# Chunk 0's transpose moved from the end of a phase to its start, in a two-layer Fourier and MLP kernel

## The chip, the cores and the metric

The kernel runs on one core of a Trainium2 chip. The core has a matrix engine (TensorE, called PE in the profile, with its weight loads as PEld), a vector engine (VectorE, DVE), a scalar engine (ScalarE, ACT), GpSimd (POOL) and a queue engine (SyncE, SP) which here issues the DMAs. The engines run side by side and wait for each other by semaphores. The metric is the device time of one execution in microseconds (us). The time before is 1433.97 us, the median of three runs (1433.92 to 1434.22).

## The reference

The sequence has 2048 rows of 512 numbers. Two kinds of layer alternate, each twice, in float32:

```
A(x): a = x @ Wd_re^T ; b = x @ Wd_im^T            # DFT along the 512
      y = Ws_re @ a - Ws_im @ b                     # DFT along the 2048, real part
B(x): h  = gelu(layernorm(x) @ w1)
      hs = [h shifted +1 | -1 | +2 | -2 rows, a quarter of the columns each] @ w2
      x1 = x + hs
      return x1 + gelu(layernorm(x1) @ w3) @ w4
x = x + A(layernorm(x)) ; x = x + B(layernorm(x))   # twice
```

So B works on a layernorm of a layernorm of x; the kernel calls that twice normed and transposed block `z`. It is the input of the product with w1.

## The kernel before

The 2048 rows are cut in NC = 4 chunks of 512 rows (CH), a chunk in TC = 4 tiles of 128 rows. `xs[0..7]` keep two tiles each in SBUF, and `xt(j)` is tile j of 16. All products are float32 in three passes (`mm3`, L279 to L281): each operand is split into a rounded high part and a low rest, and high x high, high x low and low x high are summed. A high part is a cast on ACT (`high`, L423; L225, L228, L232 for streamed pieces), a low part a subtraction on DVE (`low`, L426; L242). Three matmuls of 512 columns thus use one pair of blocks, and the second of the three (L280) is the first that reads the low part of the streamed block.

The DFT matrices and the weights come from HBM piece by piece. `issue_dma` (L207) queues a load into one of RAW = 4 `raw` buffers as soon as the buffer's last reader is done; `stage_one` takes a ring slot, and casts; `stage_two` makes the low part. There are RING = 4 ring slots. `stream()` hands the next split piece to the matmuls and first calls `prefetch`, which writes as many stages as ring slots are free. All of it is written in one program order (a manual schedule): on each engine the instructions run in the order in which the Python code emits them, and SP's queue holds the loads in that order too. A load or store that waits holds all that is queued behind it.

A layer's chunk c of the sequence DFT has an x phase (`x_phase`, steps i = 0 to 15, two for each of 8 pairs k) and a y phase (`y_phase`, two kinds for each of 8 k, `by1` and `by0`). In the y phase a piece of the stream is the difference of two raw pieces: DVE subtracts them (`ring0f` to `ring3f`, L231), ACT casts the difference (L232), DVE makes the low part (L242). One k takes four such DVE operations and uses two raw buffers. Each kind feeds 12 matmuls into two of the PSUM pairs PA to PD. At a phase's steps a `hook` emits other work: loads, norms, statistics, transposes. After the last chunk's y phase the products along the 512 follow (`hid`, four of them in HORDER, on the blocks `rr`), and then `by_pairs`, which multiplies by w1 and w2 and runs the MLP. Its first product reads z of chunk 0 from `zt[0]` (f32 name `zt0f`), whose words are those of `ay0`, `ay1` and the start of `ay5`, operands of the y phase.

Getting z of a chunk into `zt` has five parts: four norms on ACT (`normed_act`, L327, into `tmp`, `spare` or `extra`), four transposes on DVE in blocks of 32 x 32 (`turn_one`, L591, into `turned`), four stores of 256 KB to a DRAM buffer `zd` (`turn_out`, L601), one load of 1024 KB in the order that finishes the transpose (`turn_in`, L606), and the split into high and low (`z_half`). `edges(0)` then clears two columns at zt's border (a memset on DVE, L611). z of chunk 0 goes this way late in the last chunk (c = 3) of each layer; z of chunk 1 follows at once in `by_pairs`, through the tile `turned01`. The scheduled stores of other work also use SP: `w4s<-w4sum` (L1445, a sum of w4 blocks that is made at x steps 10 and 11 in `w4_sum`, words 5*AY on) and the loads of `xs` from DRAM at x steps 8, 11 and 13 (BACK).

Of the kernel before, what the change touches and what calls it, by code (L numbers as in the profile page):

```python
# [19 lines left out]
CH = 512  # L20
# [22 lines left out]
def spectral_mlp_kernel(ctx: ExitStack, tc: tile.TileContext, x, ws, hs, w1, w2, w34, out):  # L43
# [50 lines left out]
    w12 = [at(f"w12{i}", W12 + i * 4 * CH, 2, 2, CH) for i in range(4)]  # L94
    beside = at("beside", XS - 4 * D - 2 * HALO * KD * 2, 4, D, dtype=F32)
    xs = [at(f"xs{i}", XS + i * 2 * D, 2, D, dtype=F32) for i in range(NP)]
    turned01 = at("turned01", H3, KD, CH, dtype=F32)
    spare = at("spare", SPARE, 2, D, dtype=F32)
    (re0, im0), (re1, im1) = ([both(f"rr{i}{h}", RR + (2 * i + h) * 4 * CH, 2, 2, CH) for i in range(2)] for h in range(2))
# [628 lines left out]
    def by_pairs(layer, zs, xin, dst):  # L728
        act = nc.scalar.copy
        w1p = [stream(), stream()]  # L730
        edges(0)
        for q in range(TC):
            turn_one(turned01, q, zs[4 + q])
# [713 lines left out]
    for layer in range(LAYERS):  # L1447
# [4 lines left out]
        for c in range(NC):  # L1452
            if layer == 0 and c == 0:
                raws[0] = raw_at[0]
                for i in (1, 0):
                    load_x()
                    nc.sync.dma_start(raws[0][:, i], pieces[0][0][:, i])
                state["dma"] += 1
                issue_dma(2)
                load_x()  # L1460
                issue_dma()
                load_x()

                slots[0] = ring[0]
                state.update(one=1, made=1)

                def block_high(i):
                    nc.scalar.copy(ring[0][:, i, 0], raws[0][:, i])

                def block_low(i):  # L1470
                    nc.vector.tensor_tensor(
                        ring[0][:, i, 1], raws[0][:, i], ring[0][:, i, 0].bitcast(F32), op=ALU.subtract
                    )

                def second_low(i):
                    nc.vector.tensor_tensor(
                        ring[1][:, i, 1], raws[1][:, i], ring[1][:, i, 0].bitcast(F32), op=ALU.subtract
                    )

                halves = [pairs[0][:, i].rearrange("p (h d) -> p h d", h=2) for i in range(2)]  # L1480
                parts = [
                    [(halves[0][:, 1], mid[0][:, 0], 1), (halves[0][:, 0], ay[0][:, 2], 0)],
                    [(halves[1][:, 0], mid[0][:, 1], 0), (halves[1][:, 1], ay[0][:, 3], 1)],
                ]

                def part_highs(i):
                    for _, t, h in parts[i]:
                        normed(t[:, 0], xt(i)[:, h * DH : (h + 1) * DH], xp[0][i])

                def part_lows(i):  # L1490
                    for v, t, _ in parts[i]:
                        nc.vector.tensor_tensor(t[:, 1], v, t[:, 0].bitcast(F32), op=ALU.subtract)

                xp[0] = stats([xt(0)])
                block_high(1)
                block_low(1)
                part_highs(0)
                normed_act(pairs[0][:, 0], xt(0), xp[0][0])
                block_high(0)
                xp[0] += stats([xt(1)])  # L1500
                part_lows(0)
                part_highs(1)
                normed_act(pairs[0][:, 1], xt(1), xp[0][1])
                block_low(0)
                state["two"] += 1
                issue_dma()
                part_lows(1)
                xp[0] = pairs[0]
                state["limit"] = 2

                def hook(i):
                    k, odd = divmod(i, 2)
                    if not i:
                        second_low(1)
                        xp_stats(1)
                        second_low(0)
                        state["two"] += 1
                        issue_dma()
                        state["limit"] = 4
                        prefetch()  # L1520
                    state["limit"] = w_items[layer]
                    if not odd:
                        if k + 1 < NP:
                            xp_norm(k + 1, 3)
                            xp_main(k + 1)
                        if not k:
                            xp_main_lows(1)
                    else:
                        if 0 < k < NP - 1:
                            xp_main_lows(k + 1)  # L1530
                        if k + 2 < NP:
                            xp_stats(k + 2)
                        if k:
                            xp_sums(k - 1)
                            xp_highs(k - 1, False)
                            xp_lows(k - 1, False)
                    w4_split(i)

                plain_phase(hook)
                continue  # L1540

            def hook(i):
                k, odd = divmod(i, 2)
                if layer == 0 and c == 1:
                    if i == 1:
                        xp_sums(NP - 1)
                    if i == 2:
                        xp_highs(NP - 1, False)
                    if i == 3:
                        xp_lows(NP - 1, False)  # L1550
                    w4_split(2 * NP + i)
                if c == 0:
                    if layer:
                        for step, f in zip((0, 0, 1), (ay_sums, ay_highs, ay_lows)):
                            if i == step:
                                f(5)
                            if i == step + 10:
                                f(6)
                        for k, first, stages in (
                            (6, X6, (xp_stats, xp_norm, ax_sums, ax_highs, ax_lows)),  # L1560
                            (7, X7, (xp_stats, xp_norm, ax_sums, ax_highs, ax_lows)),
                        ):
                            for step, f in zip((0, 1, 3, 4, 6), stages):
                                if i == first + step:
                                    f(k)
                    return
                if (layer, c) in W4_AT:
                    w4_sums(W4_AT[layer, c], i)
                j = (c - 1) * TC
                if i == 4:  # L1570
                    rows(X1, xin, j, 2, True)
                if i == 9:
                    rows(X1, x1d, j, 2, False)
                if i == 10:
                    rows(X1, xin, j + 2, 2, True)
                if c == NC - 1 and i in BACK:
                    rows(xs[BACK[i] // 2], x1d, BACK[i], 2, True)

            x_phase(c, hook)

            def hook(k):
                if layer and c == 0:
                    for step, f in zip((1, 1, 2), (ay_sums, ay_highs, ay_lows)):
                        if k == step:
                            f(7)
                if k == 1 and c:
                    rows(X1, x1d, (c - 1) * TC + 2, 2, False)
                if c == NC - 1:
                    if k < 2:
                        for j in (2 * k, 2 * k + 1):  # L1590
                            zs[j] = tmp[:, j]
                            normed_act(zs[j], xt(j), ln2[j])
                    if k in (3, 4):
                        for q in (2 * k - 6, 2 * k - 5):
                            turn_one(turned01, q, zs.pop(q))
                    if k == NP - 2:
                        turn_out(turned01)

            y_phase(c, hook)

# [4 lines left out]
        for i, (ri, dp) in enumerate(HORDER):  # L1605
            if i == 1:
                run_late("im1")
            if i == 3:
                state["limit"] += 2
            s = stream()  # L1610
            hid(ri, dp, s, acc4, 0, i == 0, i == 3)
            if i == 0:
                turn_in(ztf[0], HALO)
            if i < 2:
                j = (6, 8)[i]
                rows(xs[j // 2], x1d, j, 2, True)
            if i == 0:
                run_late("re1", "im1+")
            if i == 1:
                run_late("re0+", "re0++")  # L1620
                for half in range(2):
                    high(z_half(0, half))
                zs.update(norm_z((4, 5)))
            if i == 2:
                run_late("re0")
                for half in range(2):
                    low(z_half(0, half))
                zs.update(norm_z((6, 7)))
        by_pairs(layer, zs, xin, out if last_layer else x2d)


# [53 lines left out]
```

## Time and profile before

| | |
|---|---|
| median of the runs | 1433.97 us |
| the profiled execution | 1435.09 us, its span 1433.0 us |
| PE busy | 1426.2 us, 100% of the span, 6285 matmuls |
| PEld, DVE, ACT, POOL busy | 82%, 82%, 51%, 6% |
| granted TensorE clock | 1.0 |
| DMA | 307.57 MB, mean 215 GB/s |

The profile is one execution. The span runs from the first to the last instruction, and 2.1 us of the profiled execution's time lie around it. A busy time is a sum over instructions; matmuls are pipelined, so one that takes 389 ns by its record starts 0.227 us after the one before. A bracket behind a row of the timeline tells how long the engine was idle before it and whose work ended that idle time. The last chunk of layer 0 has its y phase from 343.8 us to 388.9 us of the span, and `hid` from there to 411 us; in layer 1 the y phase runs from 1054.0 us to 1097.7 us, and `hid` to 1120 us.

### The profile page before, as it was taken

What the parts mean: (1) busy time and instruction counts of PE and PEld (TensorE: products, weight loads), DVE (VectorE), ACT (ScalarE), POOL (GpSimd) and SP (SyncE); (2) the same over time, 40 slices, a digit from 0 to 9 for tenths busy, and PEclk for the clock granted to TensorE, in tenths of its full rate; (3) what the DMA queues carried; (4) which work ended last, traced back from release to release, by engine and by line L of the source; (5) the groups of instructions that cost most, each with busy time, mean ns of one, the idle gap of its engine ahead of it and who ended that gap; (6) DMA issues with size and microseconds to landing.
All of it is one profiled execution on the core that took longest, in us unless ns stands there. A gap on an engine that the chain in (4) does not pass through costs nothing.

```text
span 1433.0 us, 17362 instructions
## 1 busy us (share of the span) xinstructions
PE 1426.2 (100%) x6285; PEld 1175.7 (82%) x6285; DVE 1169.2 (82%) x1632; ACT 728.6 (51%) x974; POOL 79.8 (6%) x111
## 2 busy tenths in 40 slices
PE   9999999999999999999999999999999999999998
PEld 8888888888778888888888888888888788888887
DVE  7986998988969788656789989889889687656676
ACT  6663455455465744434555544554554665343352
POOL 2100000000002000000000000000000010000000
PEclk9999999999999999999999999999999999999999
DMA  7866656657664858945656566575776458477764
GB/s 255 273 206 205 206 195 228 209 186 268 221 192 109 278 203 267 353 156 177 205 169 198 177 227 206 184 236 192 225 263 232 140 158 296 153 243 283 243 205 162
DMA packets 127829, 307.57 MB, mean 215 GB/s; under 512 B 9217, under 2 KB 50177, under 8 KB 124545
## 3 DMA queue, kind: packets, MB, share of 16 engines
q1 hardware_dynamic: 127744, 306.48, 64.5%
q8 instruction: 49, 0.80, 0.2%
q14 instruction: 36, 0.29, 0.1%
HBM read 252.18 MB, written 54.26 MB: 214 GB/s over the span
## 4 chain that ended last, share of the span: by engine, by line
PE 93%; DVE 4%; DMA 1%; ACT 1%; issue 1%; POOL 0%; SPq 0%; DVEq 0%; ACTq 0%; POOLq 0%
PE psd L279 9%; PE psd L280 9%; PE psd L281 9%; PE psa L279 8%; PE psa L280 7%; PE psa L281 7%; PE psc L280 7%; PE psc L281 7%; PE psc L279 7%; PE psb L280 7%; PE psb L279 7%; PE psb L281 7%; DMA raw<-in_ws 1%; DVE ring L242 1%; DVE xs L963 0%
## 5 line engine op out<-in xcount | busy, mean ns | idle before, releaser
L225 ACT CAST ring<-raw 128x1024 fp32r<-128x1024 f32 x127 | 133.0, 1052 | 79.9 <-PE psd L281 40.1
L242 DVE TENSOR_TENSOR ring<-raw,ring 128x1024 fp32r<-128x1024 f32 x126 | 153.4, 1219 | 14.0 <-ACT ring L225 13.8
L279 PE MATMUL psd<-ring,rr 128*128 128x512 f32 x208 | 80.9, 389 | 0.0
L280 PE MATMUL psd<-ring,rr 128*128 128x512 f32 x208 | 80.9, 389 | 0.0
L281 PE MATMUL psd<-ring,rr 128*128 128x512 f32 x208 | 80.9, 389 | 0.0
L319 POOL TENSOR_TENSOR rs<-ve,mhalf 128x4 f32<-128x4 f32 x16 | 27.8, 1737 | 611.4 <-DVE nm L318 611.4
L232 ACT CAST ring<-ring0f 128x1024 fp32r<-128x1024 f32 x28 | 29.5, 1055 | 60.0 <-DVE ring0f L231 60.0
L632 ACT ACTIVATE tmp<-rest 128x512 f32<-128x512 f32 x30 | 19.0, 632 | 73.0 <-DVE rest L465 72.7
L242 DVE TENSOR_TENSOR ring<-ring1f,ring 128x512 fp32r<-128x512 f32 (+1 forms) x56 | 53.2, 950 | 0.7 <-ACT ring L228 0.7
L280 PE MATMUL psb<-ring,ay 128*128 128x512 f32 x128 | 50.1, 392 | 1.1 <-DVE ring L242 1.1
L298 POOL TENSOR_TENSOR rs<-ve,mhalf 128x2 f32<-128x2 f32 (+1 forms) x33 | 28.2, 853 | 412.8 <-DVE nb L297 412.8
L327 ACT ACTIVATE tmp<-xs,nb,rs 128x512 f32<-128x512 f32 x56 | 43.3, 810 | 14.8 <-POOL nb L299 13.6
L281 PE MATMUL psb<-ring,ay 128*128 128x512 f32 x128 | 49.8, 389 | 0.0
L279 PE MATMUL psc<-ring,ay 128*128 128x512 f32 x128 | 49.8, 389 | 0.0
L279 PE MATMUL psb<-ring,ay 128*128 128x512 f32 x128 | 49.8, 389 | 0.0
L281 PE MATMUL psc<-ring,ay 128*128 128x512 f32 x128 | 49.8, 389 | 0.0
L280 PE MATMUL psc<-ring,ay 128*128 128x512 f32 x128 | 49.8, 389 | 0.0
L279 PE MATMUL psa<-ring,ay 128*128 128x512 f32 x126 | 49.0, 389 | 0.0
L280 PE MATMUL psa<-ring,ay 128*128 128x512 f32 x126 | 49.0, 389 | 0.0
L281 PE MATMUL psa<-ring,ay 128*128 128x512 f32 x126 | 49.0, 389 | 0.0
L279 PE MATMUL psd<-ring,ay 128*128 128x512 f32 x126 | 49.0, 389 | 0.0
L280 PE MATMUL psd<-ring,ay 128*128 128x512 f32 x126 | 49.0, 389 | 0.0
(666 smaller groups left out, 4426.4 us busy)
## 6 DMA issues: line engine op xcount, KB each, us to landing
raw<-in_ws SPq DMA_DIRECT2D x183, 512.0 KB, 4.9
w4r<-w4d SPq DMA_DIRECT2D x66, 512.0 KB, 4.4
raw<-in_hs SPq DMA_DIRECT2D x56, 512.0 KB, 3.6
w3b<-w3d SPq DMA_DIRECT2D x14, 1792.0 KB, 8.3
w3d<-w3b SPq DMA_DIRECT2D x5, 1792.0 KB, 6.8
x1d<-tmp SPq DMA_DIRECT2D x12, 512.0 KB, 6.2
xs<-x1d SPq DMA_DIRECT2D x12, 512.0 KB, 6.1
w4d<-w4in SPq DMA_DIRECT2D x11, 512.0 KB, 4.7
```

Of the source, the lines that this page charges most:

```text
L225: nc.scalar.copy(dest[:, a:b, 0], r[0][:, a:b])
L232: nc.scalar.copy(dest[:, :, 0], lo)
L242: nc.vector.tensor_tensor(lo, src, hi.bitcast(F32), op=ALU.subtract)
L279: nc.tensor.matmul(o, lh, rh, start=first, stop=False, skip_group_check=more)
L280: nc.tensor.matmul(o, lh, rl, start=False, stop=False, skip_group_check=more)
L281: nc.tensor.matmul(o, ll, rh, start=False, stop=last, skip_group_check=more)
L298: nc.gpsimd.tensor_tensor(rs[:, :n], ve[:, :n], mhalf[:, 0, :n], op=ALU.pow)
L319: nc.gpsimd.tensor_tensor(rs, ve, mhalf[:, :, :2], op=ALU.pow)
L327: nc.scalar.activation(o, s, AF.Identity, bias=mr[2], scale=mr[1])
L632: nc.scalar.activation(g_of, ps_of, AF.Gelu_apprx_tanh)
```

## The change

The transpose of chunk 0's z moves ahead, and its last steps are put in another order:

- The norms of tiles 0 to 3 move from y steps 0 and 1 of the last chunk to x steps 12 and 15.
- The four transposes move from y steps 3 and 4 to y step 0, and go to a tile of their own, `turned0`, at words 5*AY, where `w4_sum` was read out before. The stores to `zd` move from y step 6 to y step 0.
- The load of `zt[0]` moves from the first product of `hid` to the hook of y step 7.
- The high parts of z are emitted behind the first product of `hid` in place of the second. The low parts, both at the third before, are emitted at the second and the third.
- The norms of tiles 6 and 7 move from `hid` into `by_pairs`, behind the casts of w1.

No operation is added or removed.

```diff
+    turned0 = at("turned0", 5 * AY, KD, CH, dtype=F32)
     turned01 = at("turned01", H3, KD, CH, dtype=F32)
...
         w1p = [stream(), stream()]
+        zs.update(norm_z((6, 7)))
         edges(0)
...
                     rows(xs[BACK[i] // 2], x1d, BACK[i], 2, True)
+                if c == NC - 1 and i in (12, 15):
+                    for j in (0, 1) if i == 12 else (2, 3):
+                        normed_act(tmp[:, j], xt(j), ln2[j])
...
-                if c == NC - 1:
-                    if k < 2:
-                        for j in (2 * k, 2 * k + 1):
-                            zs[j] = tmp[:, j]
-                            normed_act(zs[j], xt(j), ln2[j])
-                    if k in (3, 4):
-                        for q in (2 * k - 6, 2 * k - 5):
-                            turn_one(turned01, q, zs.pop(q))
-                    if k == NP - 2:
-                        turn_out(turned01)
+                if c == NC - 1 and k == 0:
+                    for q in range(TC):
+                        turn_one(turned0, q, tmp[:, q])
+                    turn_out(turned0)
+                if c == NC - 1 and k == NP - 1:
+                    turn_in(ztf[0], HALO)
...
-            if i == 0:
-                turn_in(ztf[0], HALO)
...
             if i == 0:
                 run_late("re1", "im1+")
+                for half in range(2):
+                    high(z_half(0, half))
             if i == 1:
                 run_late("re0+", "re0++")
-                for half in range(2):
-                    high(z_half(0, half))
+                low(z_half(0, 0))
                 zs.update(norm_z((4, 5)))
             if i == 2:
                 run_late("re0")
-                for half in range(2):
-                    low(z_half(0, half))
-                zs.update(norm_z((6, 7)))
+                low(z_half(0, 1))
```

Three places show what the instruction streams look like. In the kernel after, every line number is one higher (L231 is L232) or two, and so are the numbers in the buffers' names. The first is DVE in the y phase of layer 0's last chunk, behind the low part of k = 1's first kind. Before:

```order
L242 TENSOR_TENSOR ring_179<-ring2f,ring_179 128x2x512
L231 TENSOR_TENSOR ring0f<-raw_184,raw_183 128x2x512
L242 TENSOR_TENSOR ring_181<-ring3f,ring_181 128x2x512
L231 TENSOR_TENSOR ring1f<-raw_184,raw_183 128x2x512
L242 TENSOR_TENSOR ring_175<-ring0f,ring_175 128x2x512
```

And in the changed kernel:

```order
L243 TENSOR_TENSOR ring_180<-ring2f,ring_180 128x2x512
L592 STREAM_TRANSPOSE turned_157<-tmp 128x16x32 x4
L232 TENSOR_TENSOR ring0f<-raw_185,raw_184 128x2x512
L243 TENSOR_TENSOR ring_182<-ring3f,ring_182 128x2x512
L232 TENSOR_TENSOR ring1f<-raw_185,raw_184 128x2x512
```

All four transposes now stand ahead of k = 2's first subtraction and of the low part that the matmuls of k = 1's second kind need (`ring3f`); before, two stood ahead of `ring2f` of k = 5 and two ahead of the addition to `rr00f` that precedes k = 6.

The second place is SP's queue beside it. Before, the two loads for k = 4 (`raw_183`, `raw_184`) follow those for k = 3:

```order
L207 DMA raw_185<-in_ws 128x1024
L207 DMA raw_186<-in_ws 128x1024
L207 DMA raw_183<-in_ws 128x1024
L207 DMA raw_184<-in_ws 128x1024
L198 DMA x1d<-tmp 128x2x512
```

In the changed kernel:

```order
L208 DMA raw_186<-in_ws 128x1024
L208 DMA raw_187<-in_ws 128x1024
L602 DMA zd_78<-turned_157 32x16x128 x4
L208 DMA raw_184<-in_ws 128x1024
L208 DMA raw_185<-in_ws 128x1024
L199 DMA x1d<-tmp 128x2x512
```

The four stores to `zd`, which wait for the transposes, now stand ahead of the loads for k = 4.

The third place is ACT at the end of layer 0's `hid`. Here `rr` is the last block of `hid`, `zt` is z of chunk 0, `w_144` to `w_147` are w1 and w2, and `spare` and `tmp` take the norms of tiles 4 to 7. Before:

```order
L423 CAST rr_159<-rr00f 128x2x512
L423 CAST zt_140<-zt0f 128x2x512 x2
L327 ACTIVATE spare<-xs_151,nb,rs 128x512 x2
L327 ACTIVATE tmp<-xs_152,nb,rs 128x512 x2
L225 CAST w_144<-raw_183 128x2x512
L225 CAST w_145<-raw_184 128x2x512
```

In the changed kernel:

```order
L424 CAST zt_140<-zt0f 128x2x512 x2
L424 CAST rr_160<-rr00f 128x2x512
L328 ACTIVATE spare<-xs_151,nb,rs 128x512 x2
L226 CAST w_144<-raw_184 128x2x512
L226 CAST w_145<-raw_185 128x2x512
L328 ACTIVATE tmp<-xs_152,nb,rs 128x512 x2
```

z's casts now come ahead of the cast of `rr00f`, and w1's two casts ahead of two of the norms.

## The prediction

> **What bounds the kernel now.** I read the page first, then PE's waits over the whole run, then the timelines of PE, DVE, ACT and SP around the last chunk of both layers. The page's line on the engines, and PE's waits:
>
> ```profile
> PE 1426.2 (100%) x6285; PEld 1175.7 (82%) x6285; DVE 1169.2 (82%) x1632; ACT 728.6 (51%) x974; POOL 79.8 (6%) x111
> ```
>
> ```profile
> PE psb L280 <- DVE ring L242: 1.1, 1, 1.1
> PE psd L279 <- issue: 0.2, 1, 0.2
> PE psa L279 <- issue: 0.2, 1, 0.2
> ```
>
> PE is out of work at the start of the kernel and at these three places, each of which lies in the code that changes. So the change can win these waits and hardly more, and loses whatever new wait it makes. PE's own timeline at the first, and at the second:
>
> ```profile
> 373.83 0.39 PE L279 MATMUL psb<-ring,ay 128*128 128x512 f32 x1
> 375.35 0.50 PE L280 MATMUL psb<-ring,ay 128*128 128x512 f32 x1 [1.13 <-DVE ring L242]
> 375.69 0.39 PE L281 MATMUL psb<-ring,ay 128*128 128x512 f32 x1
> ```
>
> ```profile
> 410.73 0.39 PE L281 MATMUL psb<-ring,rr 128*128 128x512 f32 x1
> 411.33 0.47 PE L279 MATMUL psd<-zt,w 128*128 128x512 f32 x1 [0.21 <-issue]
> 411.64 0.40 PE L280 MATMUL psd<-zt,w 128*128 128x512 f32 x1
> ```
>
> A matmul takes 1426.2 / 6285 = 0.227 us of PE. The first wait therefore costs 1.52 - 0.23 = 1.29 and 0.34 - 0.23 = 0.11, together 1.40 us; it is the second kind of k = 5 in layer 0. The second wait is the first product with w1 and costs 0.37 + 0.08 = 0.45 us. The third row of the waits is the same place in layer 1, for another 0.45. In all 2.30 us.
>
> **Why DVE is late at 374.** DVE in layer 0's y phase:
>
> ```profile
> 349.44 1.23 DVE L231 TENSOR_TENSOR ring0f<-raw,raw 128x1024 f32<-128x1024 f32 x1 [2.19 <-PE psa L281]
> 350.58 1.22 DVE L242 TENSOR_TENSOR ring<-ring3f,ring 128x1024 fp32r<-128x1024 f32 x1
> ...
> 360.35 1.22 DVE L231 TENSOR_TENSOR ring0f<-raw,raw 128x1024 f32<-128x1024 f32 x1
> ...
> 370.63 1.29 DVE L591 STREAM_TRANSPOSE turned<-tmp 128x512 f32<-128x512 f32 x2
> 371.85 1.18 DVE L465 TENSOR_TENSOR rr00f<-rr00f,rr11f 128x1024 f32<-128x1024 f32 x1
> ...
> 374.08 1.21 DVE L242 TENSOR_TENSOR ring<-ring3f,ring 128x1024 fp32r<-128x1024 f32 x1
> ```
>
> One operation follows another after 1.14 us (349.44 to 350.58), and two transposes take 1.22 us (370.63 to 371.85). From 349.44 on DVE has no gap, and the low part that PE waits for ends at 374.08 + 1.21 = 375.29. Ahead of it stand four transposes, 2.44 us, more than the 1.40 us of delay. Just before 349.44 DVE idled 2.19 us. In the chain of waits this gap ends where a load for k = 2 lands, at 341.95 + 7.37 = 349.32:
>
> ```profile
> 341.95 7.37 DMA raw<-in_ws
> ```
>
> **The change, part by part.**
>
> *Transposes into y step 0, layer 0.* They start where the gap starts, at 349.44 - 2.19 = 347.25, and end at 349.69. `ring0f` moves by 0.25 us, and with it all up to k = 4. From k = 5 on DVE is a pair of transposes ahead, from k = 6 on both, so k = 5's last low part ends at 375.29 + 0.25 - 2.44 = 373.1. PE wants it at 373.83 + 0.23 = 374.06. The wait of 1.40 us goes. What is late next are the loads for k = 7: their raw buffers come free a pair of transposes earlier, at most 1 us, so DVE may stand before them for up to 1 us. The low part behind that has no more than some 0.3 us of margin.
>
> *The same in layer 1*, where the loads came early and DVE idled only 0.35 us:
>
> ```profile
> 1057.87 1.23 DVE L231 TENSOR_TENSOR ring0f<-raw,raw 128x1024 f32<-128x1024 f32 x1 [0.35 <-DMA raw<-in_ws]
> 1059.01 1.22 DVE L242 TENSOR_TENSOR ring<-ring3f,ring 128x1024 fp32r<-128x1024 f32 x1
> ...
> 1065.11 1.22 DVE L231 TENSOR_TENSOR ring3f<-raw,raw 128x1024 f32<-128x1024 f32 x1 [0.34 <-PE psa L281]
> ...
> 1070.34 1.22 DVE L242 TENSOR_TENSOR ring<-ring3f,ring 128x1024 fp32r<-128x1024 f32 x1
> ```
>
> These are the matmuls that read the low parts of 1059.01 and 1070.34:
>
> ```profile
> 1062.42 0.39 PE L280 MATMUL psb<-ring,ay 128*128 128x512 f32 x1
> ...
> 1073.30 0.39 PE L280 MATMUL psb<-ring,ay 128*128 128x512 f32 x1
> ```
>
> The transposes run from 1057.52 to 1059.96, so `ring0f` is 2.09 us late. Queued behind it is the low part of k = 1's second kind, which now ends at 1059.01 + 2.09 + 1.22 = 1062.32. That leaves 0.10 us, and a handover takes 0.06 (375.29 to 375.35). Before 1065.11 the delay shrinks by the gap of 0.34, to 1.75, and the low part of 1070.34 ends at 1073.31, for a matmul at 1073.30: a wait of 0.07 us. In layer 0 the first margin is alike: 350.58 + 0.25 + 1.22 = 352.05, for a matmul at 343.8 + 3 x 2.72 + 0.23 = 352.2. So four places stand at the edge. I charge them 0.2 us together; the bounds are 0 and 4 x 0.3, as DVE can't be later than its own queue makes it.
>
> *Norms into x steps 12 and 15.* Four on ACT, none added. ACT in layer 1:
>
> ```profile
> 1050.10 1.05 ACT L232 CAST ring<-ring0f 128x1024 fp32r<-128x1024 f32 x1 [2.01 <-DVE ring0f L231]
> ...
> 1055.65 1.10 ACT L498 COPY rr00f<-psa 128x512 f32<-128x512 f32 x2
> 1056.61 1.10 ACT L232 CAST ring<-ring3f 128x1024 fp32r<-128x1024 f32 x1
> ```
>
> The first two (1.5 us, by the row at 404.94 below) fit into the gap of 2.01 us. The second two come ahead of the copies of PA and move them by 1.5 us: the first ends at 1057.7, and PE needs that half at 1054.0 + 18 x 0.227 = 1058.1. The cast of `ring3f` then ends near 1059.2, before DVE takes it at 1061.1. Their input and `turned0`'s words depend on DMAs issued four x steps or more ahead, all landed by then in the trace. No cost; were this cover gone, each us of ACT would be one of PE.
>
> *Stores to zd on SP.* They now stand ahead of the loads for k = 4. The first view shows these loads, the second the four stores, the third a load right behind the stores, all as before:
>
> ```profile
> L207 SPq DMA_DIRECT2D raw<-in_ws x2: 328/376/424, 353.0 to 353.3; - x2
> DMA to landing us min/median/max: 5.1/5.5/5.9
> ```
>
> ```profile
> L601 SPq DMA_DIRECT2D zd<-turned x4: 424/570/1200, 381.9 to 383.6; - x4
> DMA to landing us min/median/max: 6.7/7.2/7.2
> ```
>
> ```profile
> L207 SPq DMA_DIRECT2D raw<-in_w x1: 1069/1069/1069, 387.0 to 387.0; - x1
> DMA to landing us min/median/max: 5.2/5.2/5.2
> ```
>
> The four issues take 383.6 + 1.2 - 381.9 = 2.9 us. From 349.7 that is 352.6, and the loads wait for DVE until 353.2 anyway. Right behind the stores a load takes 1.07 us to issue and lands after 5.2; its partner lands 1.2 us later (353.0 + 5.1 against 353.3 + 5.9). So the pair is in at 358.4 and 359.6, and DVE needs it at 360.35 + 0.25 = 360.6. In layer 1 DVE comes there 1.75 us later than before, which leaves more. I take 0. The bounds are -0.2, since SP has no stores to issue any more ahead of w1's loads, and what the first rival prices.
>
> *z earlier at the end of `hid`.* ACT there in layer 0, then DVE:
>
> ```profile
> 401.95 1.05 ACT L423 CAST rr<-rr00f 128x1024 fp32r<-128x1024 f32 x1 [4.82 <-DVE rr00f L465]
> 402.91 2.13 ACT L423 CAST zt<-zt0f 128x1024 fp32r<-128x1024 f32 x2
> 404.94 1.52 ACT L327 ACTIVATE spare<-xs,nb,rs 128x512 f32<-128x512 f32 x2
> ...
> 407.78 3.88 ACT L225 CAST w<-raw 128x1024 fp32r<-128x1024 f32 x4
> ```
>
> ```profile
> 408.85 2.36 DVE L242 TENSOR_TENSOR w<-raw,w 128x1024 fp32r<-128x1024 f32 x2 [1.28 <-ACT w L225]
> ...
> 411.16 0.07 DVE L611 MEMSET zt<- 128x16 f32 x1
> ```
>
> What PE's list calls "issue" ends 0.1 us after the memset (411.23). The memset stands behind w1's low parts, and these behind w1's casts on ACT. In the change z's two casts (2.1 us) fill ACT's gap of 4.82, and two norms go behind w1's casts, which start 3.4 us earlier, near 404.4. The low parts and the memset end near 407.8; PE arrives at 410.73 + 0.23 = 410.96, or 409.6 with the 1.40 us won. Both layers' 0.45 go. The cast of `rr00f` waits for DVE as before and keeps its time; its low part gets one operation of z ahead of it, while ACT is still casting.
>
> **The sum.** In the profiled execution, 1435.09 us (span 1433.0), the waits are worth 2.30 us. It stands 1.12 us above the runs' median, 1433.97. The 1.40 hang on a late load that layer 1 doesn't show at the same place, so I count half of it for a timed run: -0.70 - 0.90 + 0.20 = -1.4, and 1433.97 - 1.4 = 1432.6 us. With all 2.30 and no new wait it is 1431.7, with 0.9 won and 0.5 lost 1433.6.
>
> **Rivals.**
>
> *The loads for k = 4 come late* (slower), in both layers, on SP and in the DMA engines. For it: a load issued at 332.2, behind several others, took
>
> ```profile
> DMA to landing us min/median/max: 9.0/9.0/9.0
> ```
>
> At that price the second load lands at 353.6 + 9.0 = 362.6, 2.0 us after DVE needs it, and PE has next to no margin there: 2.0 us per layer, and as much again if k = 5's loads are held up by the same queue. 1432.6 + 4.0 = 1436.6, or 1440.6 with k = 5. It outweighs the gain from 0.7 us per layer on. Against it: in the window from 350 to 353 the DMA engines did little (the last two numbers are their busy share and GB/s):
>
> ```profile
> 350.00:353.00 3.00, 3.00 (x15) 2.49 (x14) 3.00 (x4) 1.06 (x1) 0.00 (x0) 1.00 0.20 82
> ```
>
> The Trainium skill's page "DMA: Bandwidth & Descriptors" (Latency and other measured facts) gives an access to HBM as 0.2 us on average and 2 us under high load. By that rule, taken as an estimate, the pair would land up to 1.8 us later, each layer would lose up to 0.8 us, and the change would come out even, near 1434. The 5.2 us of the load right behind the stores speak against it.
>
> *The waits of before aren't in the timed runs, or come back one step on* (no change). 1.40 us shows in one layer of one execution, and four margins of 0.1 us may turn into waits of 0.3: 1433.97 - 0.9 + 1.2 = 1434.3, or with nothing lost 1433.1.
>
> *More goes than PE's list shows* (faster): 2.30 us and 0.6 or more of gaps too short for that list, 1431.0.
>
> **The numbers.** 0.2% is 2.9 us, about what a measurement of this kernel can tell from no change. The forecast has 0.63, late loads 0.17 (0.12 of it past 1436.8), waits that come back 0.15, more than the list 0.05. The range runs from 1431.3, all waits gone, to 1435.2, late loads at two thirds of their lower price. Faster 0.05, same 0.83, slower 0.12.
>
> **What would show it.** Right: PE's waits list no `psb` for `ring` and no `issue` ahead of the first product of `zt`; DVE has its transposes near 347.3 and 1057.5 and idles before a `ring` subtraction of k = 6 or 7; the loads behind the `zd` stores land by 360.6. Wrong: PE waits for `ring` between 352 and 370, or DVE waits for a load at k = 4 or 5, or PE waits for ACT's copies of PA.

## The result and the profile after

The changed kernel takes 1436.69 us (median of 22 runs, 1434.71 to 1438.08), the kernel before 1434.24 us (22 runs, 1433.72 to 1435.35). The ratio is 1.0016 with a 95% interval of 1.001 to 1.0023: a small loss of 2.45 us, where a gain of 1.4 us was forecast. The profiled execution took 1436.16 us, its span is 1434.0 us.

The page's line on the engines, then PE's waits over the whole run (us in total, times, longest):

```profile
PE 1426.2 (99%) x6285; PEld 1176.5 (82%) x6285; DVE 1169.5 (82%) x1632; ACT 728.0 (51%) x974; POOL 79.7 (6%) x111
```

```profile
PE psb L281 <- DVE ring L243: 2.3, 2, 1.4
PE psd L135 <- POOL mhalf L55: 1.4, 1, 1.4
PE psb L280 <- ACT beside L529: 0.2, 1, 0.2
```

PE has as much to do as before. Both waits that the profile called "issue", ahead of the first product with w1, are gone. In their place stand two waits for a low part (`ring`) of 0.86 and 1.44 us, and one for ACT's copies of PB (`beside`). The second row is the kernel's start, which the change doesn't touch; a fourth row of 0.2 us, left out here, lies there too. PE's timeline at the two waits for `ring`, and at the copies of PB in both layers (the listed wait of 0.2 us is layer 1's):

```profile
363.14 0.39 PE L280 MATMUL psb<-ring,ay 128*128 128x512 f32 x1
364.39 0.50 PE L281 MATMUL psb<-ring,ay 128*128 128x512 f32 x1 [0.86 <-DVE ring L243]
364.73 0.39 PE L282 MATMUL psb<-ring,ay 128*128 128x512 f32 x1
...
389.91 0.39 PE L282 MATMUL psc<-ring,rr 128*128 128x512 f32 x1
390.44 0.50 PE L280 MATMUL psb<-ring,rr 128*128 128x512 f32 x1
...
1072.72 0.39 PE L280 MATMUL psb<-ring,ay 128*128 128x512 f32 x1
1074.55 0.50 PE L281 MATMUL psb<-ring,ay 128*128 128x512 f32 x1 [1.44 <-DVE ring L243]
1074.89 0.40 PE L282 MATMUL psb<-ring,ay 128*128 128x512 f32 x1
...
1100.11 0.39 PE L282 MATMUL psc<-ring,rr 128*128 128x512 f32 x1
1100.69 0.50 PE L280 MATMUL psb<-ring,rr 128*128 128x512 f32 x1 [0.19 <-ACT beside L529]
```

With 0.227 us for a matmul, the first costs 1.25 + 0.34 - 2 x 0.227 = 1.14 us, the one of layer 1 costs 1.83 + 0.34 - 0.45 = 1.72, and the holds at the copies of PB 0.53 - 0.23 = 0.30 and 0.58 - 0.23 = 0.35. The two for `ring` are new and lie in the second kind of k = 3. At the copies of PB the kernel before had a hold of 0.1 us in each layer already (389.99 to 390.32 in layer 0). DVE shows what stood ahead of the low part there:

```profile
347.47 2.48 DVE L592 STREAM_TRANSPOSE turned<-tmp 128x512 f32<-128x512 f32 x4
...
361.97 1.23 DVE L232 TENSOR_TENSOR ring0f<-raw,raw 128x1024 f32<-128x1024 f32 x1 [1.14 <-DMA raw<-in_ws]
363.12 1.22 DVE L243 TENSOR_TENSOR ring<-ring3f,ring 128x1024 fp32r<-128x1024 f32 x1
...
375.33 1.22 DVE L232 TENSOR_TENSOR ring1f<-raw,raw 128x1024 f32<-128x1024 f32 x1 [0.78 <-PE psd L282]
```

```profile
1057.05 2.48 DVE L592 STREAM_TRANSPOSE turned<-tmp 128x512 f32<-128x512 f32 x4
...
1072.13 1.23 DVE L232 TENSOR_TENSOR ring0f<-raw,raw 128x1024 f32<-128x1024 f32 x1 [1.71 <-DMA raw<-in_ws]
1073.27 1.22 DVE L243 TENSOR_TENSOR ring<-ring3f,ring 128x1024 fp32r<-128x1024 f32 x1
```

DVE works in order. It stands 1.14 and 1.71 us before the subtraction of k = 4, whose loads haven't landed, and the low part of k = 3, whose data is long there, is queued behind that subtraction. It ends at 363.12 + 1.22 = 364.34, and PE goes on at 364.39.

The row at 375.33 is the first subtraction of k = 7 (the y phase takes it ahead of the second of k = 6). Its bracket names PE, but the second load for k = 7 lands at 370.4 + 4.8 = 375.2, just before it. In the run g1 (under the experiments) the same subtraction starts at 373.55, while PE is still at the matmuls that the bracket names (its next group starts at 373.83). So DVE waited here for the load too.

SP's four stores to `zd` in layer 0, the loads for k = 4 behind them, and the same loads in layer 1 (durations of the issue in ns, then first and last issue):

```profile
L602 SPq DMA_DIRECT2D zd<-turned x4: 330/709/1258, 350.0 to 351.9; - x4
DMA to landing us min/median/max: 2.7/4.1/4.7
```

```profile
L208 SPq DMA_DIRECT2D raw<-in_ws x2: 887/1030/1172, 353.4 to 354.6; - x2
DMA to landing us min/median/max: 7.3/7.3/7.3
```

```profile
L208 SPq DMA_DIRECT2D raw<-in_ws x2: 882/1052/1222, 1063.1 to 1064.1; - x2
DMA to landing us min/median/max: 7.6/7.8/7.9
```

The stores land from 350.0 + 2.7 = 352.7 to 351.9 + 4.7 = 356.6, so one every 1.3 us on average: 256 KB in 1.3 us is 200 GB/s. The loads behind them land at 353.4 + 7.3 = 360.7 and 361.9. Before, the same pair landed after 5.1 and 5.9 us, at 358.1 and 359.2. In windows of 1.5 us (the last two columns are the busy share of the DMA engines and GB/s) the engines are now full; before, the same two windows had shares of 0.02 and 0.68, the second with the loads for k = 4 themselves under way:

```profile
352.00:353.50 1.50, 1.50 (x8) 1.23 (x7) 1.50 (x3) 0.29 (x2) 0.00 (x0) 1.00 0.92 194
...
355.00:356.50 1.50, 1.50 (x8) 1.27 (x7) 1.50 (x2) 0.81 (x1) 0.00 (x0) 1.00 0.98 155
```

At the end of `hid` all went as planned. ACT, DVE and PE of layer 0:

```profile
397.15 2.13 ACT L424 CAST zt<-zt0f 128x1024 fp32r<-128x1024 f32 x2
...
404.45 1.98 ACT L226 CAST w<-raw 128x1024 fp32r<-128x1024 f32 x2
```

```profile
407.84 0.07 DVE L612 MEMSET zt<- 128x16 f32 x1
```

```profile
411.10 0.40 PE L280 MATMUL psd<-zt,w 128*128 128x512 f32 x1
```

w1's casts start at 404.45 and the memset ends at 407.91, 3.2 us before PE comes.

### The profile page after: what moved, and what is told of

It is laid out like the page before. It is cut to its first block, busy times and chain, and to the rows that moved or that the text cites. A ratio compares the mean times of both kernels' runs of the same rounds, so it can differ in the third digit from the quotient of the medians.

```text
span 1434.0 us, 17354 instructions
## 1 busy us (share of the span) xinstructions
PE 1426.2 (99%) x6285; PEld 1176.5 (82%) x6285; DVE 1169.5 (82%) x1632; ACT 728.0 (51%) x974; POOL 79.7 (6%) x111
## 4 chain that ended last, share of the span: by engine, by line
PE 91%; DVE 4%; DMA 2%; ACT 1%; issue 1%; SPq 0%; POOL 0%; DVEq 0%; ACTq 0%; POOLq 0%
PE psd L280 9%; PE psd L282 9%; PE psd L281 9%; PE psa L280 7%; PE psa L282 7%; PE psa L281 7%; PE psc L281 7%; PE psc L282 7%; PE psc L280 7%; PE psb L281 7%; PE psb L280 7%; PE psb L282 7%; DMA raw<-in_ws 1%; DVE ring L243 1%; DMA raw<-in_hs 0%
```

## The experiments

The theory, called D in the expectations: the four stores hold the DMA engines for some 5 us, the loads behind them land late, DVE stands before these loads, and the low part that PE wants is queued behind. Each run gives its median beside the kernel before on the same chip (1434.25 us for e1 to e4, 1434.07 for e2 again and f1 to f3, 1434.12 for g1 to g3).

| run | what it is | median us | ratio, 95% interval |
|---|---|---|---|
| e1 | after, stores at y step 4 | 1436.1 | 1.0013 [1.0004, 1.0021] |
| e2 | before, two norms behind w1's casts | 1433.23 | 0.9993 [0.9984, 1.0002] |
| e2 again | the same | 1433.44 | 0.9996 [0.9987, 1.0005] |
| e3 | after, stores in rows of 2 KB | 1434.72 | 1.0 [0.9991, 1.0009] |
| e4 | after, with the end of `hid` as before | 1438.04 | 1.0025 [1.0016, 1.0035] |
| f1 | early norms and transposes, no early stores | 1434.83 | 1.0006 [0.9996, 1.0015] |
| f2 | after without the stores | 1434.32 | 1.0001 [0.9993, 1.001] |
| f3 | after, two stores at y step 0, two at 4 | 1436.7 | 1.0016 [1.0007, 1.0025] |
| g1 | f1 with two transposes at y step 0, two at 4 | 1433.05 | 0.9989 [0.9981, 0.9998] |
| g2 | f1 with the transposes where they were before | 1433.18 | 0.9994 [0.9985, 1.0003] |
| g3 | after, eight stores | 1449.21 | 1.01 [1.0085, 1.0116] |

**The two halves apart.** First the kernel before with one move, and the changed kernel without its end:

```diff
         w1p = [stream(), stream()]
+        zs.update(norm_z((6, 7)))
         edges(0)
...
-                zs.update(norm_z((6, 7)))
```

> The kernel before with one part of the change alone: the norms of tiles 6 and 7 are emitted behind w1's casts. If the wait ahead of the first product of zt is for DVE's memset, behind w1's low parts, behind w1's casts on ACT, the casts come 1.4 us earlier and the memset ends ahead of PE: both waits go, minus 0.9 us, 1433.2 to 1433.5 us. If the wait is PE's own issue (many semaphores on one instruction), it stays, and the time is 1434.0 to 1434.4 us.

> The kernel before with only the norms of tiles 6 and 7 moved behind w1's casts, once more, to set a narrower interval on its gain: 1433.0 to 1433.6 us, about 0.9 us under the kernel before, as the two waits ahead of the first product of zt are worth 0.45 us each.

1433.23 and 1433.44 us, as expected: the two waits of 0.45 us are won by this move alone. Neither interval excludes 1. The profile of e2 has no wait for `ring` in the y phase though nothing there was changed, so the 1.40 us at 374 in the profile of before isn't a typical run's.

The second, shortened (the splits of z go back to the second and third product too):

```diff
         w1p = [stream(), stream()]
-        zs.update(norm_z((6, 7)))
         edges(0)
...
-                if c == NC - 1 and k == NP - 1:
-                    turn_in(ztf[0], HALO)
...
+            if i == 0:
+                turn_in(ztf[0], HALO)
...
             if i == 0:
                 run_late("re1", "im1+")
-                for half in range(2):
-                    high(z_half(0, half))
...
+                zs.update(norm_z((6, 7)))
```

> The changed kernel with the tail of the kernel before: norms, transposes and stores stay early, but the load of zt, its split and the norms of tiles 6 and 7 are where they were. Theory D: the new waits for ring stay at 1 us or more in each layer, and the 0.45 us ahead of the first product of zt come back twice: 1437.2 to 1438 us. If the loss of the change came from its second half (z's early load and casts, the copies of beside that PE waits for in hid), this kernel is at 1434.5 us or below.

1438.04 us: the moves in the x and y phases alone cost 3.8 us against the kernel before, and by the medians the end of `hid` wins 1.35 us of it back. The waits at k = 3 are there again, but with 0.91 and 0.50 us they are under the 1 us expected; the profiled execution, 1437.24 us, is the fastest of the nine.

**The stores moved, widened, left out, halved, doubled.**

```diff
-                    turn_out(turned0)
+                if c == NC - 1 and k == 4:
+                    turn_out(turned0)
```

> The changed kernel with one thing put back in part: the four stores to zd are issued at y step 4 (behind the loads for k = 7) instead of step 0; the transposes stay at step 0. Theory D (the stores hold the DMA engines, so the loads for k = 4 land late and DVE, standing before them, keeps back the low part of k = 3's second kind): the loads for k = 4 land about 5.5 us after issue again, PE's waits for ring vanish in both y phases, and with the two waits before the first product of zt gone as well the time is 1432.2 to 1433.2 us. Rival Q (the transposes themselves make DVE late, the stores only show it): PE still waits for ring at k = 1's or k = 3's second kind, 0.5 us or more in a layer, and the time is 1434 to 1436.5 us.

1436.1 us: missed by theory D. Rival Q has the time in its range, but not its waits: those at k = 1 and k = 3 are not in PE's list. The stores now hold up k = 7's second load, which is issued just ahead of them and lands after 6.5 us (5.1 in f1, which has no stores there). SP's loads for k = 7, DVE and PE in layer 0:

```profile
L208 SPq DMA_DIRECT2D raw<-in_ws x2: 328/612/896, 369.1 to 369.5; - x2
DMA to landing us min/median/max: 4.2/5.4/6.5
```

```profile
376.17 1.23 DVE L232 TENSOR_TENSOR ring1f<-raw,raw 128x1024 f32<-128x1024 f32 x1 [2.53 <-DMA raw<-in_ws]
```

```profile
378.59 0.50 PE L281 MATMUL psc<-ring,ay 128*128 128x512 f32 x1 [1.45 <-DVE ring L243]
```

What PE waits for is the low part of k = 6's first kind, queued behind k = 7's subtraction. So the collision is D's, at another pair of loads. In layer 1 PE loses only 0.24 us there. The rest of the loss is a wait of 0.39 us for the copies of PB in each layer. A load isn't safe because it was queued first.

```diff
-                    turn_out(turned0)
+                    count["turn"] += 1
+                    for d in range(KD):
+                        nc.sync.dma_start(zd[count["turn"] % 2][d * P : (d + 1) * P], turned0[:, d])
```

> The changed kernel, with the four stores at y step 0 writing the same 1 MB in rows of 2 KB (a tile row as it lies) instead of pieces of 512 bytes. The order of z in DRAM is then not the transposed one, so z of chunk 0 is another. Theory D with the size of the pieces as the cause: the stores hold the DMA engines for about 2.5 us in place of 5, the loads for k = 4 land by 360.6 and by 1069 or 1070, PE's waits for ring are below 0.3 us per layer, 1432.5 to 1433.5 us. If the bytes or the change from writing to reading hold the loads up, these land within 0.7 us of where they did and the time stays at 1436 or more.

1434.72 us, 2.0 us under the changed kernel and above the expectation. The stores and the loads for k = 4 in layer 0:

```profile
L1598 SPq DMA_DIRECT2D zd<-turned x4: 326/432/525, 350.9 to 352.2; - x4
DMA to landing us min/median/max: 2.5/2.9/3.1
```

```profile
L208 SPq DMA_DIRECT2D raw<-in_ws x2: 333/382/431, 354.2 to 354.6; - x2
DMA to landing us min/median/max: 4.9/5.3/5.7
```

The same bytes land from 353.4 to 355.3, one store in 0.6 us in place of 1.3, and the loads take 4.9 and 5.7 us again. So it isn't the number of bytes that holds the loads. The effect is smaller in layer 1: a store lands every 1.0 us in place of 1.2, and the loads for k = 4 take 5.9 and 6.8 us, 1 us more than in f1. PE's wait at k = 3 is gone in both layers. The edit changes two things at once: the pieces grow from 512 bytes to 2 KB, and a store reads all 128 partitions in place of 32. Which of the two makes the stores faster, no run here shows. The Trainium skill's page "DMA: Bandwidth & Descriptors" (Why small descriptors are slow) gives some 3 cycles of overhead for each packet. For 512 bytes that is, as an estimate, 19 cycles for 16; the factor of 2 measured in layer 0 is larger, so the length of the pieces alone isn't shown to be the cause.

```diff
-                    turn_out(turned0)
                 if c == NC - 1 and k == NP - 1:
-                    turn_in(ztf[0], HALO)
+                    z = x[:CH].rearrange("(d p) t -> p d t", p=P)
+                    nc.sync.dma_start(ztf[0][:, :, 1, HALO : HALO + CH], z)
```

> The changed kernel without the four stores to zd in both layers; the load of zt reads 1024 KB of x in their place, so that z of chunk 0 is other numbers of the same size. All else is as in the changed kernel. Theory D: the loads for k = 4 land by 359 and 1067.5, the waits for ring in the second kind of k = 3 go, and the run takes 1432.5 to 1433.6 us. Rival Q: the waits for ring stay, 1435.5 us or more. Rival L (the 1024 KB load of zt at y step 7 or z's casts in hid cost the time): 1435 us or more with no wait for ring in the y phase.

1434.32 us, 0.7 above D's range: without the stores 2.4 us of the loss go, and the loads for k = 4 land after 5.0 and 5.8 us. D holds for that part, and no wait for `ring` at k = 3 is left. But the run stays 0.9 us above e2, so something else costs too.

```diff
-                    turn_out(turned0)
...
+                if c == NC - 1 and k in (0, 4):
+                    z = zd[count["turn"] % 2].rearrange("(e i) t -> i e t", i=B)
+                    for b in (0, 1) if k == 0 else (2, 3):
+                        v = turned0[b * B : (b + 1) * B].rearrange("i d (a t) -> i (d a) t", a=NB)
+                        nc.sync.dma_start(z[:, :, b * P : (b + 1) * P], v)
```

> The changed kernel with two of the four stores to zd at y step 0 and two at y step 4. Theory D, by dose: two stores hold the DMA engines for about 2.6 us in place of 5.2, so the loads for k = 4 land about 1.3 us later than in the kernel before and not 2.6, near 359.4 and 360.6; DVE waits for them by 0.2 us or less, and PE's wait for ring in the second kind of k = 3 falls from 1.02 and 1.60 us to 0.4 or less in each layer. The loads for k = 7 are likewise half as late as with all stores at step 4. 1433.3 to 1434.8 us. Rival T (what counts is that stores stand ahead of the loads in the queue at all, not how long they take): waits of 1 us or more stay at one of the two places in each layer, 1435.5 us or more.

1436.7 us, no better than the changed kernel: missed by D in the time and in the dose. The wait at k = 3 is gone, but two stores at y step 0 delay k = 4's loads hardly at all: they land at 358.6 and 360.0, 0.1 and 0.4 us after f1's, where D had 1.3. These two stores have landed by 350.5 + 3.6 = 354.1, 0.6 us after the first of these loads is issued. The two at y step 4 delay k = 7's second load by about 0.9 us against f1. PE's list of f3 has the loss as small waits at four kinds of place: k = 6's first kind, behind k = 7's late load (0.8 in two), the copies of PB (0.7 in two), k = 1 in layer 1 (0.4), and the copies of PA in layer 1 (0.4). No wait of 1 us is left, so rival T's account fails too.

```diff
-                    turn_out(turned0)
+                    turn_out(turned0, zd[count["turn"] % 2])
+                    turn_out(turned0)
```

> The changed kernel with eight stores to zd at y step 0 in place of four (the first four write the same data to the other buffer). Theory D: the stores hold the DMA engines for 1.3 us each, 5.2 us more, so the loads for k = 4 land near 366 and 367 in layer 0, 5 us later than in the changed kernel; DVE then waits some 6 us for them and PE some 5 us more than in the changed kernel, in each layer; 1444 to 1448 us. Rival Q (the delay is the transposes' or a fixed cost of having stores ahead of loads in the queue): 1436.5 to 1439 us.

1449.21 us, 12.5 us above the changed kernel. PE's wait, and the eight stores in layer 0:

```profile
PE psb L281 <- DVE ring L243: 11.5, 3, 6.0
```

```profile
L602 SPq DMA_DIRECT2D zd<-turned x8: 329/1038/1492, 350.3 to 357.1; - x8
DMA to landing us min/median/max: 2.7/4.3/4.8
```

D's dose is about right here, 8.8 us of some 10: PE's waits for `ring` are 11.5 us with 0.4 at k = 1, so 11.1 at k = 3 in place of 2.3. The loads for k = 4 land at 365.1 and 366.4. The other 3.7 us, which take the run past D's range, come from a thing that D didn't contain; it is told under the last heading.

**The transposes without the stores.**

f1 is the changed kernel with stores, load and splits of z at the places that they had before. Its edit, shortened:

```diff
-                    turn_out(turned0)
-                if c == NC - 1 and k == NP - 1:
-                    turn_in(ztf[0], HALO)
+                if c == NC - 1 and k == NP - 2:
+                    turn_out(turned0)
...
+            if i == 0:
+                turn_in(ztf[0], HALO)
...
-                for half in range(2):
-                    high(z_half(0, half))
```

> The norms and the four transposes of chunk 0's z early, as in the changed kernel; the stores to zd at y step 6, the load of zt and the splits of z as in the kernel before, the norms of tiles 6 and 7 behind w1's casts. This parts the transposes' shift of DVE from the stores' hold on the DMA engines. Theory D (the stores hold the DMA engines, the loads behind them land late, and the low part that PE wants is queued on DVE behind the subtraction that waits for these loads): the loads for k = 4 land near 358 and 1066 as before, no wait for ring of more than 0.3 us in the second kind of k = 3, both waits ahead of the first product of zt gone; 1432.8 to 1433.6 us. Rival Q (the delay of DVE by four transposes is itself what PE waits for, at the places with a margin of 0.1 us): waits for ring at k = 1 and k = 3 stay, 1434.0 to 1435.5 us.

1434.83 us: above D's range, 1.4 us above e2 on the same chip, with no stores in the way. Rival Q's range holds, but not its places, as PE's list has no wait for `ring` at all. So the transposes' place costs time of its own. Where, f1 shows beside g1, which parts the transposes:

```diff
-                    if k == 0:
-                        for q in range(TC):
+                    if k in (0, 4):
+                        for q in (0, 1) if k == 0 else (2, 3):
                             turn_one(turned0, q, tmp[:, q])
```

> As the run with the early transposes alone (norms early, stores at y step 6, norms of tiles 6 and 7 behind w1's casts), but with two of the four transposes at y step 0 and two at y step 4. With all four at step 0 DVE stood 0.3 us later than in the kernel before at its last subtraction of k = 5, which frees the buffers for k = 7's loads; these landed 0.3 us later, and PE waited 0.5 us for ACT's copies of PB at the start of hid in each layer. Theory S (this net shift of DVE at k = 5, passed on by k = 7's loads, is what PE waits for there): with only two transposes ahead the shift there is 0 or negative, the waits for the copies of PB fall to 0.2 us or less, the waits at k = 1 go too since DVE is 1.2 us less late, and the run takes 1433.0 to 1433.8 us. Rival N (the norms in x steps 12 and 15, not the transposes, cost the time): 1434.4 us or more.

1433.05 us. DVE, then PE, in f1:

```profile
367.56 1.22 DVE L232 TENSOR_TENSOR ring3f<-raw,raw 128x1024 f32<-128x1024 f32 x1
...
374.42 1.23 DVE L232 TENSOR_TENSOR ring1f<-raw,raw 128x1024 f32<-128x1024 f32 x1 [1.10 <-DMA raw<-in_ws]
```

```profile
389.53 0.50 PE L280 MATMUL psb<-ring,rr 128*128 128x512 f32 x1 [0.36 <-ACT beside L529]
```

And in g1:

```profile
366.50 1.21 DVE L232 TENSOR_TENSOR ring3f<-raw,raw 128x1024 f32<-128x1024 f32 x1
...
373.55 1.23 DVE L232 TENSOR_TENSOR ring1f<-raw,raw 128x1024 f32<-128x1024 f32 x1
```

```profile
388.79 0.40 PE L280 MATMUL psb<-ring,rr 128*128 128x512 f32 x1
```

`ring3f` of k = 5 is the last reader of the buffers into which k = 7 is loaded. It is 1.06 us later in f1 (some 0.2 of it is the whole run's start), k = 7's first subtraction (`ring1f`) 0.87 us later. From there on DVE has no gap until the addition that ACT's cast of `rr10f` waits for at 385.05, and ACT has none from there to the copies of PB, for which PE waits in f1 and not in g1. So theory S holds: DVE and the loads form a loop, since a late subtraction frees its buffers late. DVE's delay goes around it, and ends at the first product of `hid` at 0.3 to 0.4 us in each layer. g1 has no wait for `ring` or for a copy in PE's list. It is the one version here that is faster than the kernel before by its interval.

> As the run with the early transposes alone, but with the transposes at y steps 3 and 4 as in the kernel before: of the early part only the four norms move, to x steps 12 and 15. Theory S: the norms cost 0 to 0.5 us, as PE may wait up to 0.5 us for ACT's copies of PA in layer 1; 1433.2 to 1434.0 us. Rival N: 1434.4 us or more.

(The edit is f1's with `k in (3, 4)` and the transposes in pairs.) 1433.18 us, as e2, and not to be told from g1: the norms in the x phase cost nothing by themselves. What stays open: f1's profiled execution took 1433.98 us, 0.85 less than its median, so its profile doesn't hold all that f1 loses; and the waits of 0.4 us at k = 1 and at the copies of PA in layer 1 stand in f3 and, smaller or alike, in f2, but not in the changed kernel's profile. They weren't followed further.

## Why the prediction was wrong

The forecast was 1432.6 us, and 1436.69 lies past its range.

- **The step that failed: "Stores to zd on SP ... I take 0."** The pair for k = 4 was put at 358.4 and 359.6; it landed at 360.7 and 361.9, where DVE was ready at 361.97 - 1.14 = 360.83. The time of DVE was right to 0.2 us, that of the loads wrong by 2.3. The 5.2 us were those of a load issued 2.2 us after its stores' issues had ended, and in the kernel before stores and loads overlap there; here the loads come at once behind stores that go alone. And the low share of 0.20 from 350 to 353 was that of a window without the stores: it says that there is room, not how long the stores fill it. Measured, the term is 1.14 + 1.72 us, and the runs without, with fewer, with longer-rowed and with more stores show that it is the stores'. It is the sign of being wrong that the prediction itself named, a wait of DVE for a load at k = 4.
- **"In layer 1 DVE comes there 1.75 us later than before, which leaves more"** was wrong as well. The loads' buffers are freed by the same DVE, so the loads were issued later too: 1063.1 for 1061.4. Layer 1 lost more, not less.
- **"What is late next are the loads for k = 7"** named the right place and gave it no price. Its margin was taken as a gain, on the ground that the buffers come free a pair of transposes earlier. The profile that the prediction read is the odd one here: counted from the phase's first matmul, k = 5's last subtraction starts after 24.6 us in its layer 0, but after 23.2 in its layer 1 and in both layers of e2 again, and after 23.5 and 23.9 in f1. So with all four transposes at the front the buffers come free later than in a typical run, not earlier. Measured, it is the hold at the copies of PB: 0.30 and 0.35 us in the changed kernel, of which the kernel before had 0.1 each, and 0.36 and 0.27 us of listed waits in f1.
- **Half of the 1.40 us.** The wait at 374 is gone from the profile, as predicted, but it wasn't in a typical timed run: both profiles of e2, with the y phase as before, lack it, and the kernel before is only 1.0 and 0.6 us above e2 by the medians of the same chip, which the two waits of 0.45 us cover. The 0.70 should have been near 0.
- **Right:** the 0.9 us at the end of `hid`, by its place, its cause and its size (e2), and the times there: w1's casts near 404.4, the memset near 407.8. By e2 the norms' move alone wins it. Right were also the transposes' places, DVE's gap at k = 7, and the norms at no cost.
- **The edges at k = 1 and k = 3, 0.20 us.** In the changed kernel k = 1 has no wait in PE's list; f2, f3 and g3 show 0.4 us there in layer 1. At k = 3 the edge can't be told from the late loads.

The first rival, late loads for k = 4, is what happened, and its 1436.6 us met the median by its sum and not by its terms: it has 2.0 us a layer for 1.14 and 1.72, starts from 0.70 us that weren't there, and lacks the copies of PB. So that it met the median is luck. Worked out from the runs it is e2's 1433.3 + 1.14 + 1.72 = 1436.2, and the holds at PB's copies, 0.20 and 0.25 us beyond those of before, lead to 1436.6, for 1436.69 measured. These terms come from one profiled execution, which took 1436.16 us, so the last half microsecond isn't shown.

## What to carry to other kernels

A load's landing time holds for the company that it had in the profile. A store put ahead of loads is priced by the time in which its pieces pass the DMA engines, taken from a place where such stores go alone (here 1.3 us for 256 KB from 32 partitions in pieces of 512 bytes). What counts is how much of that time is left when a load is issued: in the changed kernel 3.2 us were left, and the pair landed 2.2 and 2.3 us after f1's; in f3 0.6 us were left, and it landed 0.1 and 0.4 us after. In e1 a load issued just ahead of the stores was held as well. Where an engine's own work frees the buffers of its next loads, moving work ahead on it makes the loads late too: follow the delay around that loop to the end of the phase, and spread the moved work (two and two) rather than put it in one place. Spreading took the loss away here; it won nothing that g2 and e2, with the transposes at their old places, don't have.

## What the runs showed of the hardware

The clock, in g3. PE's timeline around the long wait in layer 0, and windows behind it, after that, and behind the pause of 6 us in layer 1 (the third column from the end is the granted clock):

```profile
363.50 0.39 PE L280 MATMUL psb<-ring,ay 128*128 128x512 f32 x1
368.93 0.79 PE L281 MATMUL psb<-ring,ay 128*128 128x512 f32 x1 [5.03 <-DVE ring L243]
369.52 0.63 PE L282 MATMUL psb<-ring,ay 128*128 128x512 f32 x1
369.94 0.63 PE L280 MATMUL psb<-ring,ay 128*128 128x512 f32 x1
```

```profile
368.90:374.00 5.10, 5.07 (x12) 4.01 (x13) 4.51 (x4) 2.09 (x2) 0.00 (x0) 0.50 0.56 173
374.50:380.00 5.50, 5.50 (x26) 4.53 (x25) 5.29 (x5) 2.11 (x2) 0.00 (x0) 1.00 0.61 204
...
1086.80:1091.00 4.20, 4.17 (x10) 3.30 (x11) 4.20 (x4) 1.78 (x2) 0.00 (x0) 0.50 0.45 120
```

After the pause of 5 us PE had half its clock for some 5 us: a matmul takes 0.43 us (369.52 to 369.94) and not 0.227, and 12 matmuls in 5.1 us have lost 5.1 - 12 x 0.227 = 2.4 us. In layer 1 it is 4.2 - 10 x 0.227 = 1.9 us. Together that is more than the 3.7 us that D lacks; but while PE is slow DVE catches up, and PE's list of g3 has no wait for the copies of PB. With the pauses of 0.86 and 1.44 us of the changed kernel the clock stays at 1.00, here behind the first:

```profile
364.40:368.00 3.60, 3.60 (x16) 2.99 (x17) 3.60 (x4) 1.23 (x2) 0.00 (x0) 1.00 0.40 101
```

The Trainium skill's page "TensorE: Matmul & The Clock Gate" (Part 1) says that the clock halves when PE has been idle for a window of about 3.4 us; the pause of 5 us agrees, and no run here has a pause between 1.5 and 5 us in the y phase. So a wait that grows past some length, here between 1.5 and 5 us, costs more than itself.

The second is the stores' rate: in layer 0, 256 KB to DRAM take 1.3 us from 32 partitions in pieces of 512 bytes, and 0.6 us from 128 partitions in rows of 2 KB (1.2 and 1.0 us in layer 1, by the landings).
